# The small score pieces of an attention kernel: two head groups or four in one visit of TensorE

## The chip, the cores and the metric

The kernel runs on one core of a Trainium2 chip. The metric is the time of one execution on the device in microseconds; given are the median of several runs and one execution recorded by the hardware profiler. Matmuls run on TensorE (PE), copies and products on VectorE (DVE), exponentials and copies on ScalarE (ACT), masks and some sums on GpSimd (POOL); SyncE (SP) issues nearly all DMAs.

## The reference, cut to what matters

```python
def _A_ref(x, wq, wk, wv, wo, beta):          # x: (1, 2048, 640), bf16
    H = 32; Dh = D // H; N = 4; L = S // N    # 32 heads of 20, 4 segments of 512
    ...
    mask = (ar[:, None] < ar[None, :]) * -1e9
    for s in range(N):
        logits = einsum('bhqd,bhkd->bhqk', qs, ks) * scale + mask
        a_dot = einsum('bhqk,bhkd->bhqd', softmax(logits), vs)
        a_mem = (phi(qs) @ M) / (phi(qs) @ z + 1e-6)
        o = g * a_mem + (1.0 - g) * a_dot     # g = sigmoid(beta), one per head
        M, z = M + phi(ks)^T vs, z + sum(phi(ks))
    return o @ wo
def _B_ref(x, w_r, w_i):                      # 2-D real FFT, product, inverse FFT
    return irfft2(rfft2(x) * (w_r + 1j * w_i))
g = sigmoid((x * gate_w).sum(-1))
return g * _A_ref(x, ...) + (1 - g) * _B_ref(x, ...)
```

Within a segment the attention is causal, so of the 512x512 scores of a head only those with key up to query count.

## The kernel before, in words

**Work.** Four segments are projected (`project`), read against the memory (`mem_read`), attended (`attend`) and added to the memory (`mem_update`). The FFT part (`fft`), written as matmuls with tables, fills the engines beside it. At the end the two parts meet in `finish_tile`: matmuls of the inverse FFT (`Fb`) and of the output weights (`oproj`) add up in one PSUM bank, which is copied out (`final`) and stored.

**Scores.** The 32 heads form eight groups of four. A score tile has keys on partitions and queries on columns. Per group `PIECES` names three kinds: kind 0 ("a", key block 0 and more, 512 columns a head), kind 1 ("b", 512 columns), and kind 2 ("c", 128 columns a head: the small pieces of key blocks 2 and 3). `qk_unit` is one visit: a set of small matmuls (64x64 tiles of TensorE, 20 rows deep, four heads at once) into four PSUM banks, one a head, and one `exp` on ACT from there into the tile `ex` in SBUF. All visits use the same four banks (pool "qk", banks 0 to 3), so a visit cannot begin before the exponential of the one before has read them. Kinds a and b are visits of one group (128x2048 elements for the exponential), kind c a visit of two groups (128x1024). `UNITS` gives five visits for each pair of groups, 20 a segment, 80 in all. (In segment 3 the exponentials of kinds b and c are split in two.)

**Masks.** `mask` runs `affine_select` on POOL: two masks for a, two for b, three for c, seven a group, 224 in all. Masks of kind c in segments 0 to 2 are 128x256, 128x256 and 64x512 elements.

**After the masks.** In segments 0 to 2 `pv_flipped` multiplies `ex` by the values (`pvf`, pieces from `VPIECES`), in segment 3 `pv_group` does it the other way round (`pv`), followed by three small DVE operations on `rs` (`pv_den`, `pv_rec`, `pv_mul`). `denominators` loads the sums of a segment, takes reciprocals into `dnr` (DVE) and stores them.

**Buffers.** `ex` holds three slots of 4 x 1280 columns, used in turn by the groups: a at 0, b at 576, c at 1088, copies of masked blocks at 512 and 1216. Behind it lie `on` and `mem`; the FFT's first step uses their place as `xf` until all eight `fold` steps are done. The queries and keys of half a segment (four groups) come padded from DRAM into `qkp` by four loads (`pad`), on SP's queue.

**Tilings.** TensorE works in three: the whole array (mode 0), 64x64 tiles for scores (mode 1), 32-column tiles (mode 2, for `pvf`, `Fb` and some others).

**Order.** `record` numbers 2335 operations as it goes through the code. `ORDER`, a list written out in the source, gives all of them in one sequence: each entry is twice the operation's number, plus one if the second engine of its choice is taken (copies may run on ACT or DVE, some sums on DVE or POOL). `schedule` follows it, gives out PSUM banks and semaphores, and `emit` writes each engine's instructions in that order. Nothing is reordered at run time.

Of the kernel before, what the change touches and what calls it, by code (L numbers as in the profile page):

```python
# [10 lines left out]
F32 = dt.float32  # L11
# [33 lines left out]
class Op:  # L45
    __slots__ = ("id", "alts", "preds", "succs", "prio", "banks", "nbytes", "npred", "eng", "t0", "t1",
                 "stamp", "need_inc", "dyn", "first", "outside", "name", "dma", "key", "xfer", "lock", "mode", "emode", "hold", "width", "count")


class Sched:  # L50
# [15 lines left out]
    def op(self, alts, r=(), w=(), prio=0.0, nbytes=0, name="", after=(), dma=False, xfer=0.0, lock=False, mode=0, hold=False, width=16):  # L66
# [6 lines left out]
        o.xfer, o.lock, o.mode, o.hold, o.width = xfer, lock, mode, hold, width  # L73
# [43 lines left out]
    def schedule(self, pools, order, nsem=56):  # L117
# [38 lines left out]
        issued = []  # L156
        self.order = []
# [18 lines left out]
        def head(e, port_free=False):  # L176
# [31 lines left out]
            elif e == "pool":  # L208
                t = max(t, port - self.PORT[1])
                if ldv is not None:  # L210
                    t = max(t, ldv.t1 + 35.0)
                elif pos["dve"] < len(queue["dve"]) and queue["dve"][pos["dve"]].lock:
                    x = head("dve", True)
                    if x is not None and x <= t - 50.0:
                        t = max(t, free["pool"] + 21.0)
            return t

        while len(self.order) < len(order):
# [282 lines left out]
VPIECES = ((0, 0, 512, 0), (1, 512, 384, 128), (2, 896, 192, 320), (2, 1088, 64, 256), (3, 1152, 64, 448), (3, 1216, 64, 384))  # L501
# [3 lines left out]
class Kern:  # L505
# [84 lines left out]
    def dma(self, dst, src, nbytes, r, w, prio, tr=False, name="", after=(), queue="sp"):  # L590
# [1075 lines left out]
```

## Time and profile before

| | |
|---|---|
| three runs | 236.71, 237.77, 238.03 us; median 237.77 |
| profiled execution | 237.23 us, of which the span of instructions is 235.50 |
| TensorE clock granted | 0.998 |
| score visits, exponentials | 80, 92 |
| DMA | 42.18 MB, mean 179 GB/s |

A row of a group in the profile has the source line, the engine and operation, written and read tile with their shapes, the count, then busy us and mean ns of one, then the idle time of the engine ahead of it and what ended it. L1321 is the exponential, L1342 the mask; L561 and L559 are all matmuls (the helper `mms`), L571 and L573 the copies on ACT and DVE. PEld is TensorE's weight loading, which runs beside its matmuls; the idle time of PEld is not that of PE. In a row of waits stand the total in us, the number of times and the longest. SPq is SP's queue of DMA issues. In a table of stretches each engine's busy us stand with the number of its instructions.

### The profile page before, as it was taken

The page shows a single profiled execution, that of the slowest core. Times are in us where ns is not written, and L with a number is a line of the kernel's source. Part 1 is how long each engine was busy: PE and PEld are TensorE (multiplying, and loading weights), DVE is VectorE, ACT ScalarE, POOL GpSimd, SP SyncE. Part 2 cuts the span into 40 slices and gives each one's busy share as a digit, 9 for nine tenths or more (in the row PEclk, how much of TensorE's full clock was granted, in tenths as well). Part 3 has the DMA queues.
Part 4 walks back from the last instruction along what each step waited for, and adds up shares of the span by engine and source line. Part 5 has one row for each costly group of instructions (what it writes and reads, how often), then busy time and mean ns, then how long its engine had stood idle before and what let it go on. Part 6 is the DMA issues. An engine that isn't in the chain of part 4 may idle for free.

```text
span 235.5 us, 10361 instructions
## 1 busy us (share of the span) xinstructions
PE 223.7 (95%) x4391; PEld 141.5 (60%) x4391; DVE 195.1 (83%) x486; ACT 197.2 (84%) x233; POOL 162.2 (69%) x300
## 2 busy tenths in 40 slices
PE   7789999999999999999999999899999999999994
PEld 2566566775556566555557565456554456667793
DVE  0199998889999997989998888999989996857453
ACT  2169888999999998999989999998999888798820
POOL 8053139456869976737887979777998677788840
PEclk9999999999999999999999999999999999999999
DMA  7999958998979894593887773644997784472224
GB/s 148 253 356 284 214 151 170 198 241 159 248 183 209 238 227 143 134 260 112 188 222 198 199 255 79 189 121 144 212 271 195 169 163 111 94 90 82 77 68 111
DMA packets 59265, 42.18 MB, mean 179 GB/s; under 512 B 30228, under 2 KB 55380, under 8 KB 59220
## 3 DMA queue, kind: packets, MB, share of 16 engines
q1 hardware_dynamic: 58180, 40.96, 72.0%
q8 instruction: 34, 0.56, 1.0%
q10 hardware_dynamic: 1040, 0.57, 0.9%
q14 instruction: 11, 0.09, 0.1%
HBM read 23.32 MB, written 12.30 MB: 151 GB/s over the span
## 4 chain that ended last, share of the span: by engine, by line
PE 66%; ACT 13%; DVE 8%; DMA 5%; SPq 4%; issue 2%; POOL 1%; DVEq 0%; POOLq 0%
PE psum L561 59%; ACT ex L1321 11%; PE psum L559 7%; DVE Pt L1498 2%; DMA xsb<-in_A_x_dram 2%; DMA pkn<-phk 2%; SPq L596 2%; SPq L594 2%; POOL ex L1342 1%; DVE xf L958 1%; DMA qkp<-qk_scr 1%; ACT eo L571 1%; DVE qu L573 1%; DVE Bt L573 1%; DVE phk L1143 0%
## 5 line engine op out<-in xcount | busy, mean ns | idle before, releaser
L1321 ACT ACTIVATE ex<-psum 128x2048 bf16<-128x2048 f32 (+4 forms) x92 | 138.5, 1505 | 13.9 <-PE psum L561 11.7
L1342 POOL TENSOR_SCALAR_AFFINE_SELECT ex<-ex 128x256 bf16<-128x256 bf16 (+2 forms) x224 | 118.6, 550 | 29.6 <-ACT ex L1321 6.4
L561 PE MATMUL psum<-qkp 20*64 20x64 bf16 (+5 forms) x1280 | 32.3, 270 | 4.3 <-ACT ex L1321 2.8
L561 PE MATMUL psum<-xT,wq 128*128 128x512 bf16 (+1 forms) x135 | 30.4, 380 | 1.9 <-DMA xT<-in_A_x_dram 1.4
L561 PE MATMUL psum<-xT,wk 128*128 128x256 bf16 (+1 forms) x280 | 32.0, 273 | 0.1
L561 PEld LDWEIGHTS psum<-qkp 20*64 20x64 bf16 x1280 | 13.3, 102 | 22.7 <-ACT ex L1321 16.9
L561 PE MATMUL psum<-wv,xT 128*32 128x321 bf16 (+3 forms) x390 | 26.1, 301 | 0.0
L1498 DVE TENSOR_TENSOR Pt<-psum,Wt 128x642 bf16<-128x642 f32 x32 | 25.4, 818 | 0.8 <-PE psum L561 0.6
L561 PEld LDWEIGHTS psum<-xT,wk 128*128 128x128 bf16 (+1 forms) x280 | 20.2, 97 | 5.6 <-issue 1.1
L963 POOL TENSOR_TENSOR xsb<-xf 128x320 bf16<-128x320 bf16 (+2 forms) x11 | 8.4, 772 | 21.1 <-DVE xf L958 12.5
L559 PE MATMUL psum<-wo,oU 128*32 128x320 bf16 x480 | 21.5, 300 | 0.0
L1173 DVE TENSOR_TENSOR va<-psum,ebx 128x320 bf16<-128x320 f32 x32 | 15.1, 486 | 4.2 <-PE psum L561 2.7
L573 DVE CAST ot<-psum 128x320 bf16<-128x320 f32 x22 | 10.4, 487 | 9.7 <-PE psum L559 7.0
L561 PE MATMUL psum<-big,Cp 128*128 128x321 bf16 (+1 forms) x96 | 18.0, 302 | 0.1
L561 PEld LDWEIGHTS psum<-wv,xT 128*32 128x32 bf16 (+1 forms) x390 | 14.1, 96 | 6.3 <-issue 1.3
L561 PE MATMUL psum<-big,Ac 128*128 128x161 bf16 (+2 forms) x96 | 17.8, 256 | 0.0
L561 PE MATMUL psum<-ex,va 128*32 128x64 bf16 (+3 forms) x576 | 17.6, 257 | 0.2
L958 DVE TENSOR_TENSOR xf<-xsb 128x640 bf16<-128x640 bf16 x16 | 8.1, 512 | 9.7 <-DMA xsb<-in_A_x_dram 9.7
L561 PEld LDWEIGHTS psum<-ex,va 128*32 128x32 bf16 x576 | 10.9, 96 | 8.7 <-POOL ex L1342 1.7
L561 PE MATMUL psum<-tt,Yt 128*128 128x256 bf16 (+1 forms) x96 | 15.8, 275 | 0.3 <-DVE Yt L1503 0.3
L1544 DVE TENSOR_TENSOR G<-eo,psum 128x320 bf16<-128x320 f32 x32 | 14.9, 475 | 1.2 <-ACT eo L571 0.5
L1130 ACT ACTIVATE et<-qu 128x512 bf16<-128x512 bf16 x25 | 15.4, 625 | 0.2
(98 smaller groups left out, 393.3 us busy)
## 6 DMA issues: line engine op xcount, KB each, us to landing
qkp<-qk_scr SPq DMA_DIRECT2D x28, 160.0 KB
tt<-tab_tt SPq DMA_DIRECT2D x8, 512.0 KB, 4.2
qk_scr<-qu SPq DMA_DIRECT2D x12, 256.0 KB, 2.7
u_scr<-ub SPq DMA_DIRECT2D x12, 256.0 KB, 3.0
xsb<-in_A_x_dram SPq DMA_DIRECT2D x8, 320.0 KB, 5.3
oU<-u_scr SPq DMA_DIRECT2D x15, 128.0 KB, 4.9
out_dram<-ot SPq DMA_DIRECT2D x12, 160.0 KB
Wt<-in_B_w_r_dram SPq DMA_DIRECT2D x16, 80.2 KB, 4.3
```

What stands on the lines that cost most here:

```text
L559: h = e.matmul(dst, wt, r_, start=st, stop=sp_, **{**kw, "tile_position": (0, q), "skip_group_check": True})
L561: h = e.matmul(o_, l_, r_, start=st, stop=sp_, **kw)
L573: alts["dve"] = (lambda e: e.tensor_copy(dst(), src()), 67 + 1.04 * n, 68.0)
L594: return e.dma_start_transpose(d_, s_)
L958: self.either(lambda e, r=r, op=op: e.tensor_tensor(xf.ap(r * 642, [321, 2], [1, 320]), xs.ap(o, [D, 2], [1, 320]), xs.ap(o + 320, [D, 2], ...
L963: self.either(lambda e, dst=dst, src=src, d0=d0, n=n, op=op: e.tensor_tensor(xs.ap(o + dst, [D, 2], [1, n]), xf.ap(src + d0, [321, 2], [1, ...
L1130: self.one("act", lambda e: e.activation(et.ap(0, [1, L]), qsl(), ACT.Exp), L, [qb], [b("et", pi_)], late, fix=95, name="phi_exp")
L1173: self.one("dve", lambda e: e.tensor_tensor(va.ap(i * H * VW + h0 * VW, [VW, nh], [1, DH]), self.ps(bank, 0, [DH, nh], [1, DH]), self.ebx. ...
L1321: self.one("act", lambda e, d=d, q=q: e.activation(self.ex.ap(*d), self.ps(bank, *q), ACT.Exp, scale=SC), n, [bank], [self.exb(s, 2 * pr + ...
L1342: self.one("pool", lambda e: e.affine_select(self.ex.ap(e0 + d0, [1280, 4], [1, n], np_=np_), self.ex.ap(e0 + s0, [1280, 4], [1, n], np_=np_),
L1498: self.one("dve", lambda e, ri=ri, Pt=Pt, Wt=Wt, wo_=wo_, bank=bank: e.tensor_tensor(Pt.ap(ri * 322, [644, 2], [1, KD]), self.ps(bank, 0, ...
L1544: self.one("dve", lambda e, q=q, n2=n2, bank=bank, eo=eo: e.tensor_tensor(self.G.ap(n2 * D + 639 * q, [1 - 2 * q, 320]), eo.ap(q, [1, 320] ...
```

## The change

In segments 1 and 2, kind c becomes a visit of four groups: `attend` asks for it once for each two pairs, and its exponential is 128x2048 elements. Segments 0 and 3 keep their visits. That makes 76 visits instead of 80, 88 exponentials instead of 92.

`ex` gets a new layout for segments 0 to 2: kind c of each of the eight groups has a place of its own (`exc`), reused only by the same group of the next segment; a and b keep three slots in turn (`exo`, pitch 1088); the third masked block gets three slots of 4 x 64 columns (`exm`) whose partitions 0 to 63 are set to zero once (two memsets on POOL, `zero`), and its mask writes partitions 64 to 127 only. Masks of kind c are now 64x256, 128x256 and 64x256, and are recorded after the last visit of their pair. Places of groups 4 to 7 and one of the three small slots lie where `on` and `xf` lie, so their first use follows the folds. Segment 3 keeps its old layout on the same memory and follows the readers of what it overlays (`ex3`). `dnr` now lies on the four `rs` buffers, and `pv_den` follows its readers.

`schedule` has a new rule: a POOL operation that starts at a partition above 0 (`part`) waits for the POOL operation before it, and the next one waits for it. Of the POOL queue's neighbours, 45 have such a wait.

The order is new from its second quarter on. Read by the numbering, with operations named by their place in the code: TensorE's sequence is the same for its first 312 groups of matmuls of 1073 (1069 after). TensorE changes its tiling 216 times before, 211 times after. ACT has 241 operations before, 229 after; DVE 486 and 496; POOL 296 and 296; SP 239 and 239. By stretch, DVE has 172, 110, 78, 109 and 17 operations before and 173, 108, 81, 112 and 22 after, where the stretches end at the first visit of segments 1, 2 and 3, at the last visit, and at the end. The first and the last visit of segment 3 stand at places 1661 and 2213 of the order before. The last of the four `pad` loads of segment 3's second half stands 152 places ahead of that half's first visit before and 45 after.

```diff
-VPIECES = ((0, 0, 512, 0), (1, 512, 384, 128), (2, 896, 192, 320), (2, 1088, 64, 256), (3, 1152, 64, 448), (3, 1216, 64, 384))
+VPIECES = ((0, "e", 0, 512, 0), (1, "e", 512, 384, 128), (2, "e", 896, 192, 320), (2, "c", 0, 64, 256), (3, "c", 64, 64, 448), (3, "m", 0, 64, 384))
...
+                if pool_last is not None and (o.part or pool_last.part):
+                    t = max(t, pool_last.t1 + self.HOPS["pool"]["pool"])
...
+                if pool_last is not None and (o.part or pool_last.part):
+                    o.dyn.append(pool_last)
+                pool_last = o
...
-        self.ex = T("ex", [P, self.NEX * 4 * 1280])
+        self.ex = T("ex", [P, self.ONCOL + 4 * D])
+        self.cur = self.ex.off + 2 * self.ONCOL
...
-        self.dnr = T("dnr", [P, P], F32)
+        self.dnr = T("dnr", [P, P], F32, at=self.rs[0].off)
...
+        for d, n, w in (((self.MBASE, [1, 512]), 512, "m3"), ((self.MBASE + 512, [1, 256]), 256, "m3")):
+            late = n == 256
+            self.one("pool", lambda e, d=d: e.memset(self.ex.ap(*d, np_=64), 0.0), n, [], [b("ex", k, w) for k in ((2,) if late else (0, 1))], 0.0,
+                     per=0.8, name="zero", after=[b("xf", k) for k in range(3)] * late)
...
-            for u, parts in enumerate(self.UNITS):
+            if self.wide(s):
+                units = (((0, 1, 2, 3), 2),) * (pr % 2 == 0) + (((0,), 0), ((0,), 1), ((1,), 0), ((1,), 1))
+            else:
+                units = self.UNITS
+            for u, parts in enumerate(units):
                 self.qk_unit(s, pr, u, parts)
+                if parts == units[-1]:
+                    for g in (2 * pr, 2 * pr + 1):
+                        self.masks(s, g, "c", self.texp(s, 2 * pr, u))
...
+    def wide(self, s):
+        return s in (1, 2)
...
+    EPITCH = 1088
+    EBASE = 4 * 512
+    MBASE = EBASE + 3 * 4 * 1088
+    ONCOL = MBASE + 512
...
+    def exc(self, s, g):
+        return 512 * g if g < 4 else self.MBASE + 768 + 512 * (g - 4)
+
+    def exm(self, s, g):
+        return self.MBASE + (s * 8 + g) % 3 * 256
...
+            if kind == 2:
+                d, q = (self.exc(s, g), [128, 4], [512, n], [1, 128]), (0, [512, 4], [128, n], [1, 128])
+            else:
+                d, q = (e0 + 576 * kind, [self.EPITCH, 4], [1, 512]), (0, [512, 4], [1, 512])
...
-                self.mask(s, g, P, 1216 if s < 3 else 1152, sh, 64, ("c0",), ("m3",), prio, 64)
-                self.mask(s, g, P, sh, sh, 64, (), ("c0",), prio, 0)
-                self.mask(s, g, 64, 1152, 1152, P, (), ("c0", "m3"), prio, *((0, -512) if s < 3 else (-64, 64)))
+                self.mask(s, g, 64, (m0, [64, 4]), (c0, cp), 64, ("c0",), ("m3",), prio, 0, 64)
+                self.mask(s, g, P, (c0, cp), None, 64, (), ("c0",), prio, 0)
+                self.mask(s, g, 64, (c0 + 64, cp), None, 64, (), ("c0",), prio, 0)
...
-                     [bank, b("g1", s)], [dgb], prio, name="pv_den")
+                     [bank, b("g1", s)], [dgb], prio, name="pv_den", after=[b("dnr")])
```

Left out of the diff: the list of the order, the rest of the addressing that follows from the layout, and segment 3's forms, which are as before.

More of the change, by code (lines that the diff above doesn't have):

```diff
@@ L46 @@
     __slots__ = ("id", "alts", "preds", "succs", "prio", "banks", "nbytes", "npred", "eng", "t0", "t1",
-                 "stamp", "need_inc", "dyn", "first", "outside", "name", "dma", "key", "xfer", "lock", "mode", "emode", "hold", "width", "count")
+                 "stamp", "need_inc", "dyn", "first", "outside", "name", "dma", "key", "xfer", "lock", "mode", "emode", "hold", "width", "count", "part")
 class Sched:
@@ L156, in schedule @@
         issued = []
+        pool_last = None
         self.order = []
@@ L1317, in qk_unit @@
-        for n_, (d, q) in enumerate(outs):
-            n = 4
-            for x in q[2:]:
-                n *= x[1]
-            self.one("act", lambda e, d=d, q=q: e.activation(self.ex.ap(*d), self.ps(bank, *q), ACT.Exp, scale=SC), n, [bank],
-                     [self.exb(s, 2 * pr + (n_ if kind == 2 and s == 3 else gp), ks + str(n_ * (kind == 1))) for gp in gps], prio - self.QK_LEAD, name="exp" + str(n_)[n_ == 0:])
-        for gp in gps:
-            g = 2 * pr + gp
+        e0, n = self.exo(s, g), len(gps)
@@ L1325, in qk_unit, with masks @@
+        if kind < 2:
+            for gp in gps:
+                self.masks(s, 2 * pr + gp, ks, prio)
+    def masks(self, s, g, ks, prio):
+        e0, c0, m0 = self.exo(s, g), self.exc(s, g), self.exm(s, g)
+        ep = [1280 if s == 3 else self.EPITCH, 4]
+        cp = [P, 4]
+        if s < 3:
             if ks == "a":
-                self.mask(s, g, P, 512, 0, 64, ("a0",), ("m1",), prio, 64)
-                self.mask(s, g, P, 0, 0, P, (), ("a0",), prio, 0)
+                self.mask(s, g, P, (e0 + 512, ep), (e0, ep), 64, ("a0",), ("m1",), prio, 64)
+                self.mask(s, g, P, (e0, ep), None, P, (), ("a0",), prio, 0)
@@ L1342, in mask @@
+    def mask(self, s, g, np_, d, q, n, rk, wk, prio, base, p0=0):
+        d = (*d, [1, n])
+        q = d if q is None else (*q, [1, n])
         self.one("pool", lambda e: e.affine_select(
-            self.ex.ap(e0 + d0, [1280, 4], [1, n], np_=np_), self.ex.ap(e0 + s0, [1280, 4], [1, n], np_=np_),
-            [[0, 4], [step, n // 64], [1, 64]], ALU.is_ge, 0.0, base=base, channel_multiplier=-1), 4 * n, [self.exb(s, g, k) for k in rk],
-            [self.exb(s, g, k) for k in wk], prio, per=0.793, fix=218, name=f"mask{d0}" + "bc"[np_ == P])
+            self.ex.ap(*d, p0=p0, np_=np_), self.ex.ap(*q, p0=p0, np_=np_), [[0, 4], [1, n]], ALU.is_ge, 0.0, base=base, channel_multiplier=-1), 4 * n,
+            [self.exb(s, g, k) for k in rk], [self.exb(s, g, k) for k in wk], prio, per=0.793, fix=218, name="mask")
+        self.Sc.ops[-1].part = p0 > 0
@@ L1385, in pv_group @@
                 rs.ap(0, [4, 4], [1, 4], [0, DH]), ALU.mult), 320, [bank, rsb], [b("on", g)], prio, name="pv_mul",
-                after=[b("xf", k) for k in range(3)] if g == 0 else ())
+                after=[b("xf", k) for k in range(3)] * (g == 0) + [b("exc", k) for k in range(4, 8)] + [b("ex", 2, "m3")])
             if s > 0:
```

65 lines of the change are left out of this document (43 added, 22 removed), and 195 rows, old and new, of the table ORDER.

## The prediction

> **What bounds the kernel now.** I read the page's shares first, then the chain that ended last, then a table of the stretches that the chain separates, then the waits in two of them.
>
> ```profile
> PE 223.7 (95%) x4391; PEld 141.5 (60%) x4391; DVE 195.1 (83%) x486; ACT 197.2 (84%) x233; POOL 162.2 (69%) x300
> 37.63 26.45 PE psum L561 x415
> 64.08 34.84 PE psum L561 x573
> ...
> 146.86 1.89 ACT ex L1321
> 148.79 0.51 PE psum L561 x8
> 149.31 1.89 ACT ex L1321
> ...
> 37.60:79.80 42.20, 42.17 (x723) 26.76 (x724) 39.31 (x104) 40.11 (x49) 30.36 (x61) 1.00 0.96 206
> 79.80:128.20 48.40, 46.69 (x833) 28.81 (x841) 44.43 (x110) 45.95 (x50) 34.91 (x69) 1.00 0.74 189
> 128.20:168.00 39.80, 37.85 (x725) 22.53 (x724) 36.44 (x80) 37.49 (x41) 33.04 (x64) 1.00 0.58 168
> 168.00:193.00 25.00, 24.02 (x476) 13.25 (x464) 23.95 (x64) 23.14 (x29) 19.89 (x36) 1.00 0.85 202
> 193.00:222.00 29.00, 29.00 (x893) 19.91 (x886) 19.04 (x49) 23.60 (x25) 23.82 (x42) 1.00 0.50 95
> ```
>
> The columns of the last five rows are the length, then PE, PE's weight loads, DVE, ACT, POOL busy. From 37.6 to 99 us the chain never leaves TensorE. Later it alternates: one exponential, one score visit of TensorE, the next exponential, because all visits share the same four PSUM banks. From 193 to 222 TensorE is busy for 29.00 of 29.00 us. So the whole middle is TensorE work, and in part the loop between TensorE and ACT; DVE (36.44 of 39.80 in the third stretch) has little room either. POOL has 13.5 us free in the second stretch and 6.8 in the third. Counting the 80 score visits in their order gives the segments their times:
>
> ```profile
> L1321 ACT ACTIVATE ex<-psum x92: 597/1877/1887, 13.1 to 222.2; 128x2048 bf16<-128x2048 f32 x56, 128x1024 bf16<-128x1024 f32 x12, 128x1280 bf16<-128x1280 f32 x8, 128x768 bf16<-128x768 f32 x8
> 79.86 1.88 ACT L1321 ACTIVATE ex<-psum 128x2048 bf16<-128x2048 f32 x1
> 168.27 2.08 ACT L1321 ACTIVATE ex<-psum 128x1280 bf16<-128x1280 f32 x2 [0.30 <-PE psum L561]
> ```
>
> Segment 1's exponentials run from 79.86 to the narrow one at 127.06 (below), segment 2's follow, segment 3's first is at 168.27 and its last at 222.2. The change acts between 80 and 175.
>
> **Four visits fewer.** Segments 1 and 2 have four small-piece visits each now, two after the change. Matmuls and rows of scores stay as they are (each 64x64 piece is still computed once), so TensorE loses only what a visit costs beyond them: the change of tiling going in and coming out, and the wait for the banks.
>
> ```profile
> 84.44 0.16 PEld L561 LDWEIGHTS psum<-qkp 20*64 20x64 bf16 x12 [0.27 <-ACT ex L1321]
> 84.80 0.11 PEld L561 LDWEIGHTS psum<-xT,wk 128*128 128x128 bf16 x2 [0.20 <-issue]
> PEld psum L561 <- ACT ex L1321: 3.4, 10, 0.8
> PEld psum L561 <- issue: 3.5, 15, 0.4
> PEld psum L561 <- ACT ex L1321: 5.7, 16, 0.9
> PEld psum L561 <- issue: 1.6, 8, 0.2
> PE psum L561 <- ACT ex L1321: 1.4, 4, 0.6
> ```
>
> The first two rows are one visit: 0.27 us without a weight load before it, 0.20 behind it. Then come the waits of 79.8 to 127.9 us (two rows) and of 127.9 to 168 (three). Together they are 3.4 + 5.7 + 1.4 = 10.5 us going in and 3.5 + 1.6 = 5.1 coming out, over 37 visits: 0.42 us a visit. Four visits give 1.7 us. But these are eight changes of tiling, and the new order of TensorE has only five fewer in all (211 for 216): three come back between other work. At 5.1/23 = 0.22 us each that returns 0.7. **TensorE's own term is thus -1.0 us.**
>
> A rule of the Trainium skill bears on this (page TensorEngine Tiling (Array Packing), Tiling Modes, Key Properties): changing the tiling mode, not merely the tile, drains TensorE. The gaps of 0.27 and 0.20 us agree with it. By that rule alone the count of switches would be the whole gain, 5 x 15.6/74 = 1.05 us, an estimate from this page's rule and the rows above.
>
> Where the loop with ACT is the bound, a visit is worth more than its gaps. Its price is the distance between starts of exponentials:
>
> ```profile
> 127.06 1.02 ACT L1321 ACTIVATE ex<-psum 128x1024 bf16<-128x1024 f32 x1
> 128.64 1.88 ACT L1321 ACTIVATE ex<-psum 128x2048 bf16<-128x2048 f32 x1
> ...
> 133.55 1.02 ACT L1321 ACTIVATE ex<-psum 128x1024 bf16<-128x1024 f32 x1
> 135.33 1.88 ACT L1321 ACTIVATE ex<-psum 128x2048 bf16<-128x2048 f32 x1
> ...
> 144.40 1.88 ACT L1321 ACTIVATE ex<-psum 128x2048 bf16<-128x2048 f32 x1
> 146.86 1.88 ACT L1321 ACTIVATE ex<-psum 128x2048 bf16<-128x2048 f32 x1
> L1321 ACT ACTIVATE ex<-psum 128x2048 bf16<-128x2048 f32 x56 | 105.1, 1876 | 8.9 <-PE psum L561 7.5
> L1321 ACT ACTIVATE ex<-psum 128x1024 bf16<-128x1024 f32 x12 | 12.3, 1023 | 1.1 <-PE psum L561 0.8
> ```
>
> Two narrow visits take 1.58 + 1.78 = 3.36 us of the loop, a full one 2.46: 0.90 us saved for each pair that becomes one. (On ACT alone it is 2 x 1.023 - 1.876 = 0.17.) The wide exponential is not in the trace, but it has as many elements as the 2048 form, from the same PSUM shape, so I take its 1.88. With segment 2's two pairs at 0.90 and segment 1's two at 0.42, less the 0.7 that comes back, the gain is 1.9 us. Ends: nothing (the gaps come back in other places), and four times 0.90 less 0.7, that is 2.9. TensorE is 96% busy in the second stretch and 95% in the third, so I stay nearer to its own term of 1.0 than to 1.9, and take **-1.3 us**.
>
> **Masks.** Each of the 24 groups of segments 0 to 2 keeps three masks on its small pieces, but the 64x512 one halves; the new one that begins at partition 64 waits for the POOL instruction before it and makes the next one wait: 45 such places.
>
> ```profile
> L1342 POOL TENSOR_SCALAR_AFFINE_SELECT ex<-ex 128x256 bf16<-128x256 bf16 x128 | 57.8, 463 | 19.3 <-ACT ex L1321 5.9 <-ACT Cp L571 3.8 <-DVE phk L1143 2.4
> L1342 POOL TENSOR_SCALAR_AFFINE_SELECT ex<-ex 64x512 bf16<-64x512 bf16 x64 | 41.9, 662 | 6.5 <-DVE phq L1142 1.6 <-DVE phq L1143 1.4 <-DVE fbg L1080 1.4
> 165.75 0.06 issue
> 140.93 2.11 POOL L1342 TENSOR_SCALAR_AFFINE_SELECT ex<-ex 64x512 bf16<-64x512 bf16 x4 [0.34 <-DVE phq L1143]
> PEld psum L561 <- POOL ex L1342: 1.2, 4, 0.4
> L943 POOL MEMSET va<- 128x2832 bf16 x2 | 4.9, 2458 | 0.0
> ```
>
> The halving saves 24 x (0.662 - 0.463) = 4.8 us of POOL. No wait of POOL for itself is in the trace; between 0.06 us (the step between two POOL pieces of the chain) and 0.34 (a wait for another engine) the 45 cost 2.7 to 15.3 us. I take 0.1, the nearer to a step on one engine: 4.5. The two new memsets, 768 columns at 2.458/2832 us each column, cost 0.7 us, one at the start and one near 42 us, in the stretch where POOL is busy for 30.36 of 42.20. POOL stays about even, and even the dear end puts two thirds of 10.5 us into 20.3 us of idle time of two stretches: no cost. Behind a waiting mask stand the next masks and, through them, the weighted sums; if POOL's cover were gone, TensorE's wait for masks (1.2 us in the third stretch) might double.
>
> **Layout, buffers, order.** The small pieces get a place for each of eight groups, reused a segment later; the weighted sums that read the old contents stand four or more visits ahead in the new order: nothing. The reciprocal of segment 2's denominators now lies on the small buffers of segment 3's normalization, which must follow it on DVE; the order has that work five DVE operations ahead: nothing, and if its load is late, DVE waits there as now. The order hands work from ACT (229 for 241, four of them exponentials) to DVE (496 for 486). At 195.1/486 = 0.40 us, DVE gains about 4 us: five operations after the last visit, three in the stretch 168 to 222, where 11 us are free, three in segment 2, where 3.4 are free, and two fewer in segment 1. I cost it at nothing; without that idle time it would be 1.2 us in segment 2.
>
> **Sum.** The profiled execution took 237.23 us (span 235.50); -1.3 gives 235.9. The median of the three runs shown, 237.77, lies 0.54 above it, so I forecast **236.5** for the median.
>
> **Rivals.** *The loop decides everywhere.* If each pair gives 0.90, the gain is 2.9: 234.9. For it: the alternation from 121 us on. Against it: 61 us of unbroken TensorE before 99. *The gain is spent inside.* DVE and ACT run at 92 to 95% in the segments concerned, all engines run in a fixed order, and a visit that comes earlier only waits sooner; what is gained is idle time on ACT: 237.7. For it: ACT's idle in the third stretch is only 2.3 us and DVE's 3.4. *A load comes late (slower).* The loads of the padded queries and keys of segment 3's second half go from 152 places of the order ahead of their first visit to 45, past loads of sums (`oU`) and of reciprocals, a transpose and a store on SP's queue. The list runs 552 places in the 54 us of segment 3 (168 to 222), so 4.4 us remain.
>
> ```profile
> qkp<-qk_scr SPq DMA_DIRECT2D x28, 160.0 KB
> oU<-u_scr SPq DMA_DIRECT2D x15, 128.0 KB, 4.9
> u_scr<-ub SPq DMA_DIRECT2D x12, 256.0 KB, 3.0
> wo<-in_A_wo_dram SPq DMA_DIRECT2D x1, 800.0 KB, 6.9
> ```
>
> This load's own landing is not listed. Its neighbours land in 3.0 to 4.9 us, a large one in 6.9: the wait is 0 to 2.5 us there, and TensorE, with that visit at its head, issues nothing behind it; after 193 us it has no idle time to win that back. From a landing of 5.7 us on (4.4 + 1.3) the change is slower; at 6.9, 237.77 - 1.3 + 2.5 = 239.0.
>
> **How the numbers follow.** Forecast 0.45, loop everywhere 0.11, spent inside 0.17, load late 0.27. Within 0.5% (1.2 us, about what a measurement of this kernel can tell from no change) lies the span 236.6 to 239.0. The forecast's middle is just outside it: I give 0.29 of it to faster and 0.16 to no change. The loop adds 0.11 to faster; spent inside gives 0.13 to no change and 0.04 to slower, the load 0.25 and 0.02. Faster 0.40, same 0.31, slower 0.29. The range reaches from the loop's 234.9 and the load's 239.0 by 0.3 to 0.4 outward for the spread of the runs: 234.6 to 239.4. The forecast alone, with its ends of 0.7 and 1.9 us of gain, is 235.9 to 237.1.
>
> **What would show it.** Right: 60 exponentials of the 2048 form (56 + 4), 4 of the 1024 form, all near 1.88 and 1.02; TensorE's waits for the exponential and for issue down by 1 to 2 us between 80 and 168; the last exponential about 1.3 us earlier than 222.2, with TensorE still full behind it. Masks of 64x512 down from 64 to 40, POOL within 5 us of 162. Wrong: a wide exponential clearly above 1.9 us; a wait of TensorE for a load of the padded tile before segment 3's second half; POOL waiting for itself at 0.3 us or more with TensorE behind it; or the first exponential of segment 3 no earlier than now, which would mean the gain was spent inside.

## The result, and the profile after

| | median us | runs | against before |
|---|---|---|---|
| before, beside it | 238.03 | 5 (236.71 to 239.29) | |
| changed | 245.91 | 5 (244.14 to 249.89) | 1.0303 (1.0259 to 1.0347) |
| changed, again (`after_again`) | 246.96 | 4 (246.78 to 247.45) | 1.0374 (1.0332 to 1.0416) |

The change costs 3 to 4 per cent, some 8 to 9 us. The ratios, and the medians of the experiments below, leave out executions more than 1.5% above the fastest of their kernel, a slower state into which some executions of any kernel fall; the first profiled execution (249.89 us) is one. So the profile read here is that of the second series: span 244.49 us, 8.99 more than before, at a granted clock of 1.0. In it stand first the busy times and the shares of the chain that ended last, then the stretches at the cuts of the prediction.

```profile
PE 225.4 (92%) x4393; PEld 140.8 (58%) x4406; DVE 193.8 (79%) x496; ACT 193.8 (79%) x221; POOL 148.9 (61%) x300
PE 54%; DMA 19%; DVE 13%; SPq 7%; ACT 3%; issue 3%; DVEq 0%
...
37.60:79.80 42.20, 38.97 (x687) 25.08 (x690) 36.59 (x99) 37.99 (x48) 27.54 (x63) 1.00 0.95 195
79.80:128.20 48.40, 45.93 (x860) 27.14 (x858) 42.38 (x109) 45.08 (x46) 30.70 (x67) 1.00 0.64 167
128.20:168.00 39.80, 37.29 (x698) 22.18 (x685) 35.28 (x77) 35.92 (x38) 28.75 (x59) 1.00 0.62 174
168.00:193.00 25.00, 23.67 (x407) 12.52 (x404) 21.61 (x63) 22.02 (x23) 18.80 (x37) 1.00 0.77 197
193.00:222.00 29.00, 26.14 (x736) 17.38 (x740) 19.92 (x51) 20.77 (x24) 20.03 (x37) 1.00 0.62 117
```

Before, DMA held 5% of the chain and TensorE 66%; now it is 19 and 54. TensorE, idle for 0.03, 1.71, 1.95, 0.98 and 0.00 us in these stretches before, is idle for 3.23, 2.47, 2.51, 1.33 and 2.86. One row for all that follows 38 us, of before and of after, says where the whole difference lies:

```profile
38.00:235.50 197.50, 189.63 (x3900) 120.23 (x3892) 169.30 (x417) 173.41 (x197) 145.90 (x274) 1.00 0.70 169
```

```profile
38.00:244.50 206.50, 190.16 (x3896) 119.06 (x3907) 168.55 (x427) 170.34 (x186) 132.94 (x274) 1.00 0.67 162
```

TensorE's busy time is the same within 0.6 us (189.63, 190.16); its idle time went from 7.87 to 16.34. This is not a dearer visit, but 8.5 us of new waiting. Where it waits, the timeline tells:

```profile
78.85 0.25 PEld L567 LDWEIGHTS psum<-va,pkn 128*128 128x128 bf16 x4 [2.63 <-DMA pkn<-phk]
93.05 0.69 DVE L579 CAST qu<-psum 128x512 bf16<-128x512 f32 x1 [1.37 <-DMA qk_scr<-qu]
144.09 0.60 ACT L577 ACTIVATE ub<-psum 128x512 bf16<-128x512 f32 x1 [0.95 <-DMA u_scr<-ub]
192.41 0.42 DVE L1647 TENSOR_TENSOR oU<-oU,r 128x512 bf16<-128x512 bf16 x1 [1.68 <-DMA oU<-u_scr]
194.04 0.10 PEld L567 LDWEIGHTS psum<-big,Cp 128*128 128x128 bf16 x1 [1.94 <-DVE G L1606]
203.47 0.43 DVE L1647 TENSOR_TENSOR oU<-oU,r 128x512 bf16<-128x512 bf16 x1 [1.33 <-DMA oU<-u_scr]
204.35 0.11 PEld L567 LDWEIGHTS psum<-big,Cp 128*128 128x128 bf16 x2 [1.28 <-DVE ot L579]
```

Five stops behind a transfer, 8.0 us in all, on three engines: a transposed block of keys (`pkn`), two buffers whose store had not landed, two loads of sums (`oU`). The rows of 194.04 and 204.35 show how a load of sums reaches TensorE: VectorE stands at its load, and TensorE stands at the next product of VectorE. On TensorE itself three stops show, 2.63, 1.94 and 1.28 us of its weight loads, 2.42, 1.60 and 1.18 us of its matmuls: 5.2 of the 8.5 us. The rest is in shorter waits, not traced here. Before, no such stop after 37 us was longer than 0.7 us. The exponentials fall behind mostly in steps at such places (start in us; the last three columns are experiments told below):

| visit | before | after | eight_earlier | new_order_sp_early | sp_early_old_r |
|---|---|---|---|---|---|
| segment 0, last | 77.25 | 79.94 | 78.40 | 78.11 | 77.59 |
| segment 3, first | 168.27 | 173.21 | 171.43 | 170.02 | 169.23 |
| segment 3, group 3, b | 196.41 | 202.12 | 198.59 | 197.52 | 197.56 |
| segment 3, group 5, a | 199.11 | 206.28 | 204.54 | 203.25 | 201.60 |
| last | 220.97 | 229.67 | 229.62 | 228.00 | 225.79 |

The very first exponentials start at 13.13, 13.41, 13.60, 12.59 and 12.16 us, so a difference of under 1 us in this table says little.

SP's queue gives one reason. It issues in the order written out, and a transfer whose data aren't ready holds all behind it. Its largest wait of before, then two of its larger ones of after:

```profile
SPq L596 <- PE psum L561: 10.5, 10, 3.0
```

```profile
SPq L602 <- PE psum L567: 24.3, 10, 5.5
...
SPq L600 <- DVE ub L579: 7.4, 1, 7.4
```

### The profile page after: what moved, and what is told of

It is laid out like the page before. It is cut to its first block, busy times and chain, and to the rows that moved or that the text cites. A ratio compares the mean times of both kernels' runs of the same rounds, so it can differ in the third digit from the quotient of the medians.

```text
span 248.0 us, 10401 instructions
## 1 busy us (share of the span) xinstructions
PE 227.5 (92%) x4406; PEld 141.1 (57%) x4406; DVE 194.6 (78%) x496; ACT 194.0 (78%) x221; POOL 149.6 (60%) x300
## 4 chain that ended last, share of the span: by engine, by line
PE 44%; DMA 21%; DVE 17%; SPq 10%; ACT 4%; issue 2%; DVEq 0%
PE psum L567 39%; SPq L602 7%; PE psum L565 5%; DMA wv<-in_A_wv_dram 4%; DMA pkn<-phk 3%; ACT ex L1367 3%; DMA o_scr<-mem 3%; DMA tt<-tab_tt 2%; SPq L600 2%; DVE Pt L1560 2%; DMA qk_scr<-qu 2%; DVE Bt L579 2%; DMA r<-r_scr 2%; DMA qkp<-qk_scr 2%; DVE mem L1225 2%
## 5 line engine op out<-in xcount | busy, mean ns | idle before, releaser
L1404 POOL TENSOR_SCALAR_AFFINE_SELECT ex<-ex 128x256 bf16<-128x256 bf16 (+3 forms) x224 | 105.3, 488 | 46.2 <-ACT ex L1367 8.1
L1367 ACT ACTIVATE ex<-psum 128x2048 bf16<-128x2048 f32 (+1 forms) x56 | 101.7, 1816 | 11.4 <-PE psum L567 10.4
L1358 ACT ACTIVATE ex<-psum 128x1280 bf16<-128x1280 f32 (+3 forms) x32 | 36.2, 1131 | 10.7 <-PE psum L567 10.2
L567 PE MATMUL psum<-xT,wk 128*128 128x256 bf16 (+1 forms) x280 | 32.7, 273 | 0.0
L567 PE MATMUL psum<-wv,xT 128*32 128x321 bf16 (+3 forms) x385 | 27.1, 301 | 0.6 <-DVE qu L579 0.4
L567 PEld LDWEIGHTS psum<-wv,xT 128*32 128x32 bf16 (+1 forms) x385 | 13.4, 96 | 8.8 <-issue 2.7
L567 PE MATMUL psum<-big,Ac 128*128 128x160 bf16 (+2 forms) x96 | 17.4, 261 | 0.3 <-DVE Bt L579 0.2
L567 PE MATMUL psum<-tt,Yt 128*128 128x256 bf16 (+1 forms) x96 | 16.9, 277 | 0.6 <-DVE Yt L1565 0.6
L579 DVE CAST Bt<-psum 128x322 bf16<-128x322 f32 x29 | 15.0, 523 | 2.4 <-PE psum L567 2.2
L567 PE MATMUL psum<-Bt,tt 128*128 128x321 bf16 x64 | 14.1, 309 | 2.2 <-DMA tt<-tab_tt 1.5
```

Source lines behind the costliest of these rows:

```text
L567: h = e.matmul(o_, l_, r_, start=st, stop=sp_, **kw)
L579: alts["dve"] = (lambda e: e.tensor_copy(dst(), src()), 67 + 1.04 * n, 68.0)
L1358: self.one("act", lambda e, d=d, q=q: e.activation(self.ex.ap(*d), self.ps(bank, *q), ACT.Exp, scale=SC), (2048, (1280, 768)[x], 512)[kind ...
L1367: self.one("act", lambda e, d=d, q=q: e.activation(self.ex.ap(*d), self.ps(bank, *q), ACT.Exp, scale=SC), 2048 if kind < 2 else 512 * n, [ ...
L1404: self.one("pool", lambda e: e.affine_select(self.ex.ap(*d, p0=p0, np_=np_), self.ex.ap(*q, p0=p0, np_=np_), [[0, 4], [1, n]], ALU.is_ge, ...
```

## The experiments

**Which part of the change costs?** Three kernels split it: the layout alone, the wide visit in the old order, and the new order without a wide visit.

`layout_only`: the changed code, but no segment with wide visits, and the order of before with the two new memsets.

```diff
-        return s in (1, 2)
+        return s in ()
-    ORDER = (...the new one)
+    ORDER = (...the old one, two memsets more)
```

> New layout, new masks with their POOL waits, but score visits of two groups everywhere and the old order (the two memsets put in). If the new order is the cause: 237 to 239 us, no different from before. If masks and POOL waits are the cause: 242 us or more, POOL busy beyond 162 us or TensorE waiting for masks by several us more than 1.7.

Measured: 237.36 us (236.16 to 238.90, 10 runs), ratio 0.9994 (0.9954 to 1.0034). The buffers, the layout, the memsets and the waits of POOL for itself (43 in this order, 45 in the new one) cost nothing together.

`wide_old_order`: the wide visit at the place of the first narrow one in the old order, the second taken out.

```diff
-    ... c(0,1) ... c(2,3) ...
+    ... c(0,1,2,3) ... ...
```

> The whole change except the order: the wide visit stands where the first of its two narrow ones stood in the old order, the second is taken out, all else keeps the old order. If the new order is the cause: 235.5 to 239 us (my forecast's own -1.3 or, as the order was not made for it, up to 1 us more). If the wide visit itself is the cause: 242 us or more, with waits around the wide exponentials.

Measured: 241.48 us (240.10 to 242.71, 3 of 4 runs), ratio 1.0111 (1.0042 to 1.0181), between the two ranges expected. It is slower by itself, by some 1%. Below are the exponentials around one pair, of `layout_only` and then of this kernel:

```profile
112.65 1.88 ACT L1354 ACTIVATE ex<-psum 128x2048 bf16<-128x2048 f32 x1
115.02 1.02 ACT L1354 ACTIVATE ex<-psum 128x1024 bf16<-128x1024 f32 x1
116.63 1.88 ACT L1354 ACTIVATE ex<-psum 128x2048 bf16<-128x2048 f32 x1
...
124.08 1.88 ACT L1354 ACTIVATE ex<-psum 128x2048 bf16<-128x2048 f32 x1
126.46 1.02 ACT L1354 ACTIVATE ex<-psum 128x1024 bf16<-128x1024 f32 x1
128.04 1.88 ACT L1354 ACTIVATE ex<-psum 128x2048 bf16<-128x2048 f32 x1
```

```profile
115.82 1.87 ACT L1354 ACTIVATE ex<-psum 128x2048 bf16<-128x2048 f32 x1
118.54 1.88 ACT L1354 ACTIVATE ex<-psum 128x2048 bf16<-128x2048 f32 x1 [0.33 <-PE psum L567]
120.99 1.88 ACT L1354 ACTIVATE ex<-psum 128x2048 bf16<-128x2048 f32 x1
...
128.44 1.88 ACT L1354 ACTIVATE ex<-psum 128x2048 bf16<-128x2048 f32 x1
132.12 1.88 ACT L1354 ACTIVATE ex<-psum 128x2048 bf16<-128x2048 f32 x1 [0.38 <-PE psum L567]
```

From the full exponential ahead to the one behind it takes 3.98 us with a narrow visit and 5.17 with the wide one: 1.19 more. Where the second narrow visit stood, 3.96 becomes 3.68: 0.28 back. The four pairs give 0.94, 1.19, 1.05 and 1.05 at the first place and 0.49, 0.28, 0.09 and 0.08 back. The place that lost its visit hardly shrinks: TensorE is busy there for 3.96 of 3.96 us with the visit and for 3.68 of 3.68 without it, with other work. At the place that gained it is idle for 1.03 of 5.17 us, where it was idle for 0.14 of 3.98. It waits there for the banks, that is, for an exponential: the waits of TensorE's matmuls for L1354 come to 5.2 us in the whole kernel (8 times, up to 1.2), and to 2.1 us in `layout_only`. So in the old order a pair that becomes one costs about 0.8 us, four of them 3.3 us. The two medians lie 4.1 us apart, the two traces 6.4; of the latter 2.1 us stand ahead of the first wide visit (segment 1's first exponential at 81.52 against 79.45), the rest was not traced.

`narrow_new_order`: the new order, each wide visit split into two narrow ones in a row.

```diff
-    ... c(0,1,2,3) ...
+    ... c(0,1) c(2,3) ...
```

> The new order and layout, but each wide visit is split into two narrow ones that follow each other at its place. If the new order is the cause: 245 to 249 us, the changed kernel's time and up to 2 us for the four visits. If the wide visit is the cause: 237 to 240 us.

Measured: 250.45 us (250.19 to 253.28, 3 of 4 runs), ratio 1.0553 (1.0472 to 1.0634), above the range expected. `after_again`, the changed kernel on the same chip:

> The changed kernel once more, for a second profile. If transfers that land later than the new order allows are the cause, the same places stall again: TensorE behind the transposed keys (pkn) near 73 us, behind the store of the memory's part (o_scr) near 167, and behind the last chain of reciprocals near 200; 244 to 247 us, with 8 us or more of the chain in DMA. If the first profile only showed chance delays, the places differ and the total stays. If a lower granted clock of TensorE is the cause, the clock is 0.98 and every TensorE stretch is 2% longer, without waits for DMA.

Measured: 246.96 us, as above. The total stays; of the three places named, the keys stop TensorE again, the store of the memory's part costs 0.4 us, and near 200 it is loads of sums, not reciprocals. So the late transfers are in part others from one execution to the next.

In the new order the wide visit saves 3.5 us; the order itself, with narrow visits, costs 13.1 against `layout_only`. In the two traces the exponentials behind the four places are 1.05, 0.66, 0.85 and 0.67 us sooner with the wide visit, 3.2 in all, or 0.8 a pair. A lower clock does not explain the changed kernel's loss (its four runs of this series took 246.84, 247.08, 246.78 and 247.45 us at 1.0, 0.995, 0.98 and 0.976). In `narrow_new_order` it may have a small part: all four runs were granted 0.973 to 0.981.

**Is it the transfers?** Only SP's queue was changed next, then the other way round.

`eight_earlier`: eight transfers moved up in SP's queue.

```diff
 SP:
-  ...the new order's sequence
+  ...the same, but pad 14 places up, st_o 8, ld_g 4, ld_u 4; st_qk, st_o, st_u, pad 1 each
```

> The changed kernel; alone on SP's queue, eight transfers (of nearly 300) are issued earlier, by 1 to 14 places: a load of padded keys and one of queries, a store of queries, two stores of outputs, the load of the first gate, a store of sums and a load of sums. All other engines keep the new order. Theory A (the loss is late transfers: SP issues them in an order that stands still at its head, and the engines, in fixed orders too, stop at what lands late; in the changed kernel's undisturbed profile the engines' largest stops behind a transfer are 2.63, 1.37, 0.95, 1.68 and 1.33 us, 8.0 in all, and the last exponential is 8.7 us later than before): the stops behind these eight shrink, about a third to a half of 9 us comes back, 241 to 244 us. Rival B (the order of TensorE, VectorE and ScalarE is what costs, and the stops only show it): 246 to 248 us, as before this edit. Rival C (the wide visit itself costs, wherever it stands): 246 to 248 as well.

Measured: 242.65 us in the one run at a clock of 1.0, inside theory A's 241 to 244; 246.90, 247.57 and 248.12 us in three at 0.968 to 0.976. One run gives no usable ratio. The profile is that of the 246.90 us. By the table of visits 3.5 of the 5.7 us are back at group 3 of segment 3 (198.59 against 202.12), and all are lost again by the end. But between lies a stretch that the changed kernel's profile does not have:

```profile
200.72 0.76 DVE L1634 TENSOR_TENSOR oU<-oU,r 128x512 bf16<-128x512 bf16 x2 [2.01 <-DMA r<-r_scr]
201.94 0.11 PEld L567 LDWEIGHTS psum<-big,Cp 128*128 128x128 bf16 x2 [2.22 <-DVE ot L579]
202.01:212.25 10.24, 10.24 (x221) 6.18 (x225) 6.56 (x19) 4.25 (x4) 5.61 (x8) 0.50 0.25 60
```

VectorE stands for the reciprocals, TensorE behind it, and then the granted clock, the number after the five engines, is 0.50 for 10.24 us. The same stop comes up again in the next kernel.

`new_order_sp_early`: SP's whole sequence sorted anew, all other engines as in the new order.

```diff
 SP:
-  ...the new order's sequence
+  ...the same transfers, issued with more time ahead of their use
```

> The changed kernel with SP's whole sequence sorted anew, so that loads, transposes and stores are issued with more time ahead of their use; TensorE, VectorE, ScalarE and GpSimd keep the new order, instruction by instruction. Theory A (late transfers): most of the loss comes back, 238 to 242 us, and SP's longest stand behind one instruction falls below 5 us. Rival B (the order of the computing engines): 245 to 248 us, although the transfers are issued earlier. Rival C (the wide visit): 245 to 248 us.

Measured: 244.49 us (244.25 to 247.00, 4 runs), ratio 1.0289 (1.0211 to 1.0367): 2.5 us of theory A's 5 to 9, and below rival B's 245. The interval overlaps that of the changed kernel (1.0332 to 1.0416), so by the time alone the two aren't told apart. The table says more. At group 3 of segment 3 it is 1.1 us behind the kernel before, where the changed one is 5.7 behind; then 4.1 at the next visit and 7.0 at the last. Between the first two of these visits lies this:

```profile
191.00 0.36 SPq L602 DMA_DIRECT2D r_scr<-rc  x1
...
196.23 0.56 SPq L602 DMA_DIRECT2D r<-r_scr  x1
SPq L602 <- DMA r_scr<-rc: 2.7, 1, 2.7
```

```profile
198.56 0.43 DVE L1634 TENSOR_TENSOR oU<-oU,r 128x512 bf16<-128x512 bf16 x1 [1.47 <-DMA r<-r_scr]
...
200.61 0.13 PEld L567 LDWEIGHTS psum<-big,Cp 128*128 128x128 bf16 x2 [2.14 <-DVE ot L579]
```

```profile
198.00:200.00 2.00, 0.57 (x16) 0.21 (x8) 0.69 (x2) 1.90 (x3) 0.00 (x0) 1.00 0.60 179
200.00:202.00 2.00, 1.39 (x24) 1.03 (x25) 0.70 (x3) 0.00 (x0) 1.77 (x4) 0.55 0.67 182
...
210.00:211.00 1.00, 1.00 (x44) 0.44 (x40) 0.12 (x1) 0.04 (x1) 0.91 (x1) 0.79 0.73 164
```

The reciprocals of segment 2 go through HBM: SP waited for their store until 5.2 us after its issue, the load behind it could be issued only then, VectorE stood for it, and TensorE behind VectorE for 2.14 us. In the last three rows the granted clock falls to 0.50 and stays there for some 10 us, with TensorE busy for 9.80 of 10.24. From group 5's a to the visit two further on it takes 7.71 us (203.25 to 210.96); the changed kernel, with the same order on the computing engines and its clock at 1.0, takes 5.27 (206.28 to 211.55). One late transfer was paid twice, by this trace.

`sp_early_old_r`: the same kernel, the load of segment 2's reciprocals reading those of segment 1.

```diff
-    dap(self.rd.ap(), s * H * L, ...), ... [b("rd", s)]
+    dap(self.rd.ap(), min(s, 1) * H * L, ...), ... [b("rd", min(s, 1))]
```

> The kernel new_order_sp_early (244.49 us) with one dependence taken away: the load of segment 2's reciprocals (r) reads the place in HBM where segment 1's were stored long before, so it needn't wait for the store of segment 2's, which took 5.2 us to land (191.0 to 196.2 us). Segment 2's normalization therefore uses segment 1's reciprocals; nothing else changes. In new_order_sp_early VectorE stops 1.47 us for this load, TensorE 2.14 us behind it, and then TensorE's granted clock is 0.50 for some 10 us; from the visit before (197.5 us, 1.1 us later than in the kernel before) to 211.0 (6.7 us later) 5.6 us are lost. Theory A (one late transfer, and the clock that the stop costs): the stop of 2 us goes, the clock stays at 1.0, and the time falls by 3.5 to 5.5 us, to 239 to 241 us. Rival B (the order of TensorE, VectorE and ScalarE there is what costs): they run into the next wait at the same place, and the time falls by under 1.5 us, to 243 us or more.

Measured: 241.73 us (240.97 to 242.45, 4 runs), ratio 1.0202 (1.0118 to 1.0287), clock 1.0 in the profiled run. It is 2.8 us faster, less than theory A's 3.5 and more than rival B's 1.5; the interval overlaps that of `new_order_sp_early`. The next visit starts 1.65 us sooner (201.60 against 203.25) and the second behind that, with the clock at 1.0, 4.1 sooner (206.86 against 210.96); 1.9 of it is lost again by the last visit. At the place itself a wait for sums took over, 1.2 us long:

```profile
198.78 0.42 DVE L1634 TENSOR_TENSOR oU<-oU,r 128x512 bf16<-128x512 bf16 x1 [1.20 <-DMA oU<-u_scr]
```

`sp_early_old_ru`: the loads of sums too from segment 1, three of the six loads issued earlier.

```diff
-    dap(self.ud.ap(), (s * 1024 + 4 * c) * L, ...), ... [b("ud", s, i) ...]
+    dap(self.ud.ap(), (min(s, 1) * 1024 + 4 * c) * L, ...), ... [b("ud", min(s, 1), i) ...]
```

> As sp_early_old_r (241.73 us), but the five loads of segment 2's sums (oU) too read segment 1's, stored long before, and three of segment 2's six loads are issued earlier on SP's queue: the reciprocals' by 18 places, two of the sums' by 6 and 7. Segment 2's normalization thus uses segment 1's sums and reciprocals; the computing engines' order is that of the changed kernel, instruction by instruction. In sp_early_old_r VectorE still stops 1.08 us (187.85) and 1.20 us (198.78) for loads of sums, with 1.34 and 1.15 us of TensorE behind them. Theory A: these two stops go, and 1.5 to 2.5 us with them, 239 to 240.5 us; what is left above 237.4 (layout_only) is then the order of the computing engines and smaller stops. Rival B (the engines run into the next wait): 241 us or more. If nearly all of the rest were late transfers of this one place: 238.5 or less.

Measured: 241.28 and 242.91 us at clocks of 0.986 and 0.988, 245.25 and 245.53 us at 0.973 and 0.976, ratio 1.0158 (1.0065 to 1.0251). Theory A's 239 to 240.5 was not reached; rival B's 241 or more holds. The profile is that of the 245.53 us. In it the stops at loads are gone, and the next transfer stands in their place, the store of an output block whose buffer VectorE needs:

```profile
198.72 0.49 DVE L579 CAST ot<-psum 128x320 bf16<-128x320 f32 x1 [4.10 <-DMA out_dram<-ot]
...
199.27 0.10 PEld L567 LDWEIGHTS psum<-G,fbg 128*32 128x32 bf16 x4 [1.89 <-DVE ot L579]
```

Here too the clock is at 0.50 behind the stop, from 201.22 to 211.46. Three kinds of transfer hold up the same 5 us of the order, one behind the other; to take the latest away uncovers the next.

`old_order_late`: narrow visits, the old order, eleven transfers issued later.

```diff
 SP:
-  ...the old sequence
+  ... st_o 30 places down, ld_W 10, ld_r 8, st_u 6, st_o 6, ld_u 6, st_qk 5, ld_u 5, st_r 4, ld_r 1, pad 1
```

> The other way round: narrow visits and the old order of all computing engines, with the new layout (alone 237.4 us); on SP's queue eleven transfers are issued later, by 1 to 30 places, about as late against their use as in the new order. No wide visit is in it. Theory A: the time rises to 240 to 245 us, with stops of 1 to 3 us behind transfers that were not there before. Rivals B and C: 237 to 238 us, since neither the order of the computing engines nor the visits changed.

Measured: 239.84 us (238.49 to 240.61, 3 of 4 runs), ratio 1.0062 (0.9983 to 1.0141): by its time not told apart from no change, and between the two ranges. Its span is 3.5 us above that of `layout_only` (238.1 to 234.6), of which 1.2 stand already ahead of 42 us, and TensorE's longest new stop is 1.04 us behind a product of VectorE (184.58). Theory A's stops of 1 to 3 us behind transfers are not there. The old order takes late issues better than I thought.

**Can it be mended?** `wide_replanned`, `wide_margin` and `narrow_margin` sort the order of all engines anew by a plan, the last two with landing times that scatter as measured.

```diff
-    ORDER = (...the new order; for narrow_margin the old one)
+    ORDER = (...moves on all engines: of 0 to 15 places on the computing ones, of up to 42 on SP)
```

> Wide visits as in the changed kernel, with an order of all engines sorted anew from the changed kernel's: few moves on the computing engines, many on SP's queue, so that the transfers have more time. Theory A: what was lost comes back and the visits' own gain remains: 235 to 239 us. Rival C (the wide visit costs wherever it stands, 1 us for each as in the old order): 241 to 243 us. Rival B: anything from 237 to 248, by how far the moves on the computing engines happen to mend them.

Measured: 241.38 us (240.74 to 243.17, 3 of 4 runs), ratio 1.0150 (1.0066 to 1.0235).

> Wide visits, with an order of all engines sorted anew from that of wide_replanned, now with landing times of transfers that scatter as the traces of these runs show them (the same kind of store or load lands within 2 to 6 us), so that no use stands close behind its transfer. Theory A: few stops behind transfers are left, no drop of the clock behind one, and the wide visit's own gain (about 1 us of TensorE for four visits) shows at last: 235 to 239 us. Rival C (a wide visit costs about 1 us, wherever it stands): 240 us or more. Rival B: no forecast between 236 and 246.

Measured: 240.90 and 243.16 us at clocks of 0.999 and 0.99, 247.17 and 248.65 us at 0.982, with no usable ratio. Neither of the two reaches theory A's 235 to 239. Both lie where rival C put them (241 to 243, 240 or more), but so does the next kernel, which has no wide visit, so they don't speak for rival C.

> The control to wide_margin: narrow visits and the new layout, starting from the old order, sorted anew in the same way. If the margin of the transfers is all that separates the orders (theory A), there is little to win here, since the old order's stops behind transfers are 0.7 us at most: 235.5 to 238 us, and wide_margin beats it by no more than 2 us. If the sorting itself is worth much, apart from wide visits, this kernel falls to 234 us or less. If sorting by such a plan harms by itself (rival B), it rises to 240 us or more, as the new order did.

Measured: 240.60 us (238.95 to 241.57, 4 runs), ratio 1.0148 (1.0052 to 1.0244): slower than the order it started from, as rival B had it, though no wide visit is in it. Rows of the whole after 38 us, of `wide_margin`, then of `narrow_margin`:

```profile
38.00:239.20 201.20, 189.86 (x3907) 119.53 (x3899) 168.36 (x428) 169.09 (x183) 133.89 (x276) 1.00 0.71 166
```

```profile
38.00:239.00 201.00, 191.47 (x3892) 120.54 (x3884) 166.99 (x416) 172.40 (x197) 134.93 (x279) 1.00 0.69 166
```

TensorE is idle for 11.34 and 9.53 us, against 7.87 before. Of what `narrow_margin` loses there, 1.7 us are idle time and 1.8 us TensorE's busy time (191.47 against 189.63); but the traces of `layout_only` and of before, which have the same matmuls, also differ by 1.7 us in it (222.0 and 223.7 in the whole span). It is not clear of late transfers either: its exponentials fall 1.3 us further behind those of `layout_only` at one place, where a store holds a buffer (VectorE waits 1.59 us at 199.73).

No version beats the kernel before.

**What is shown, and what isn't.** Shown: the order loses, not the layout; a wide visit costs 0.8 us a pair in the old order and saves 0.8 in the new. In part shown: what in the order loses. SP's sequence and the wait for one store make up some 4 of the 9 us between the changed kernel and `layout_only`, by the ratios to the kernel before that ran beside each (1.0374, 1.0289, 1.0202, and 0.9994). The intervals of the first and the third don't overlap; those of neighbours do, and the changed kernel's first series (1.0259 to 1.0347) overlaps the third too. Not shown: what the other 5 consist of. The crowded stretch at 197 to 202 us, where three transfers wait behind one another, has a part in it; the order of the computing engines may have one, which no run here shows by itself. They were not separated: the old sequence of SP with the new one of the other engines would deadlock, and the reverse too, so neither was tried.

## Why the prediction was wrong

*Forecast 236.5, range 234.6 to 239.4, faster at 0.40; measured 245.91.* The step that failed is the term "Layout, buffers, order", the order's hand-over of work above all: "I cost it at nothing". In its place the runs showed that the order, with narrow visits, costs 13.1 us (`narrow_new_order` against `layout_only`), and that TensorE's waiting after 38 us grows from 7.87 to 16.34 us. I counted what moved between ACT and DVE and checked the one move of a load that looked long. I didn't ask, of every transfer in the new order, how long before its use it is issued; which part of the loss that question would have found is shown only for some 4 us.

*A load comes late (0.27, 239.0).* The mechanism was right in kind; place and number were wrong. I looked at the padded queries and keys of segment 3's second half, 45 places ahead. TensorE's waits for such loads (`qkp`) come to 0.3 us in all (0.4 of its weight loads). The late ones were transposed keys, sums, reciprocals and stores that free a buffer. I priced one stop at up to 2.5 us; there were five of 0.95 to 2.63 us, on three engines. A count of places also told nothing on SP's queue, where a place can last 7.4 us. The first stop, read in the rows of SP, shows what it needed. The transposed keys are issued at 70.25 in `layout_only` and at 72.40 in the changed kernel. There they landed at 78.8, 6.4 us after their issue; 2.63 us of that TensorE stood. The use had been put 3.8 us behind the issue, inside the spread of such landings (3.0 to 6.4 us in these two kernels, the kernel before, `eight_earlier` and `new_order_sp_early`).

The Trainium skill (page DMA: Bandwidth & Descriptors, section Anatomy of one DMA) puts a fixed cost of about 2 us on a transfer, most of it the receipt of the write, and warns that it can be long when the target is HBM. That section is on transfers issued by GpSimd. The store of 32 KB that SP waited for until 5.2 us after its issue, written to HBM by SP's queue, agrees with the warning and not with the 2 us; an earlier one of the same kind in that trace landed in 2.3 us.

*TensorE's own term, -1.0.* Gaps at the visits in the windows of the prediction, in and out:

```profile
PEld psum L567 <- ACT ex L1367: 3.7, 13, 0.5
PEld psum L567 <- issue: 3.6, 16, 0.4
PE psum L567 <- issue: 0.5, 3, 0.2
PE psum L567 <- ACT ex L1367: 0.4, 2, 0.2
...
PEld psum L567 <- ACT ex L1367: 3.5, 11, 0.9
PEld psum L567 <- issue: 2.5, 12, 0.3
PE psum L567 <- ACT ex L1367: 0.8, 2, 0.6
```

These are 15.0 us. The prediction's 15.6 for before leaves out one row of its first window, `PE psum L561 <- ACT ex L1321: 0.6, 2, 0.4`; with it the sum is 16.2, and the difference -1.2. Both sums add waits of weight loads to waits of matmuls, which overlap; on the matmuls alone they are 2.0 and 1.7. And the same windows hold other visits now, which start 2 to 5 us later. So these rows can't tell whether -1.0 was the right size; the visits tell more (0.8 us a pair, below). What it left out was that a gap saved at the second visit is worth nothing where other work stands (0.08 to 0.49 us, measured in `wide_old_order`), and that twice the matmuls in one visit wait longer for the banks (0.94 to 1.19).

*0.90 us a pair in the loop.* Right in the loop and not for the kernel: with the pair standing together, the change from two narrow to one wide gave 0.66 to 1.05 us a pair, 3.2 for four. In the old order the pairs do not stand together, and the sign turns. So the sign of this step hung on the order, and I took one price for both.

*The wide exponential, 1.88.* Right:

```profile
L1367 ACT ACTIVATE ex<-psum 128x2048 bf16<-128x2048 f32 x52 | 97.6, 1877 | 7.1 <-PE psum L567 6.0
L1358 ACT ACTIVATE ex<-psum 128x2048 bf16<-128x2048 f32 x8 | 15.0, 1877 | 4.3 <-PE psum L567 4.2
```

60 of this form, as forecast.

*Masks and layout at nothing.* Right: `layout_only` is at 0.9994. POOL fell from 162.2 to 148.9 us busy, where I had said about even, within 5: the masks alone fell by 14.0 (118.6 to 104.6), where I had counted 4.8. The 45 waits of POOL for itself don't show as waits at all.

*Spent inside (0.17).* ACT and DVE did not absorb a gain; there was none to absorb. *Loop everywhere (0.11)*: it needed an order that doesn't stall. The three that named faster or equal shared one assumption, that the new order runs as tightly as the old one, and 0.73 of the chances hung on it.

## What to carry to other kernels

When an order is written out for all engines, a new one has to be read transfer by transfer: the time from issue to first use against the spread of landings in the trace, not their median, and where the queue's head stands still. A merged visit saved time here only where the two stood together; elsewhere its price was the extra work at one place, and the gain at the other was hidden by what stands there. A change that brings its own order is best split at once into the new form in the old order and the old form in the new order.

## What the runs showed of the hardware that I had not expected

A stop of TensorE of 2.1 us was followed by 10.24 us at a granted clock of 0.50 in `new_order_sp_early`, although TensorE was busy for 9.80 of them; `eight_earlier` and `sp_early_old_ru` show the same length behind stops of 2.2 and 1.9 us. Behind a stop in `narrow_new_order` it was 3.41 us. In the 3.41 us ahead of these four drops TensorE was busy for 1.80, 1.28, 1.94 and 2.21 us. In the changed kernel stops of 2.63 us (at 78.85) and 1.94 us (at 194.04) were not followed by any, though TensorE was busy for only 1.65 us from 74.79 to 78.21 and 1.80 us from 190.85 to 194.26.

The Trainium skill (page TensorE: Matmul & The Clock Gate, Part 1) states that the clock halves after an idle window of about 3.4 us and is full again after a busy one as long, and that the windows run freely. The lengths of the drops, 3.41 us and three times as much, agree with such windows; that stops of about 2 us sufficed and that 10 busy us passed in three traces before the clock returned do not agree with those figures. Why some stops of this size trip it and others don't stays open.

A drop of 10.24 us stretched the same two visits from 5.27 and 5.26 us (changed kernel, `sp_early_old_r`) to 7.71, 7.82 and 7.82. In the whole time of the changed kernel a lower clock did not show.
